# Packing 64 times of two channels on the 128 contraction rows of a Toeplitz convolution that runs beside attention

## The chip, the cores and the metric

One core of one Trainium2 chip. The metric is the device time of one execution in microseconds (us), median of several. Engines: PE is TensorE (PEld its weight loads), ACT is ScalarE, DVE is VectorE, POOL is GpSimd, SP issues DMAs. A run counts as slow when it is more than 1.5% above the fastest run of the same kernel in its session; ratios use the other, fast, runs. "L541" is line 541 of the kernel that the profile belongs to.

## The reference

Two independent parts whose outputs are joined on the last axis.

```python
# A: attention, S = 2048, D = 512, 32 heads of 16
qkv = x @ wqkv ; scores = q k^T / 4 ; p = softmax(scores) ; a = (p v) @ wo
# B: long convolution, 512 channels, 2048 times
k_shift = 4-tap causal shift convolution of k with shift_k
kv = k_shift * v
y[t, d] = sum over s <= t of kv[s, d] * ssm_k[d, t - s]  +  kv[t, d] * ssm_D[d]
b = q * y
```

`ssm_k` is about 0.05/45 in size. The convolution's own share of the output is so small that most kernels with a wrong convolution still pass the comparison.

## The kernel before

A small scheduler in the kernel's source places all instructions of the five engines by modelled times, which fixes the order of each engine's queue.

There are 2,048 blocks of 128 x 512 exponentials. ACT computes 1,836 of them in 741 ACTIVATEs over two or three PSUM banks each (L541). DVE takes the other 212 with a polynomial: one FX, three EH and one PTD instruction each. PE computes the scores (QK, L530), the products with v (L623), the projections, the convolution (L795), and short fillers in the gaps of its work (L996).

The convolution is a Toeplitz product. The filters are reversed, padded and stored in DRAM (`kz_scratch`). A load with a step of one element per partition gives each partition its own shifted window. Weights are columns of `kv`, one column for each block of 128 times.

```python
KV = sb("KV", [128, NB, C])                      # time in block, block (NB = 16), channel (C = 512)
WR = sb("WR", [128, R_W, S])                     # R_W = 12 filter rows: three slots of four channels
...
src = bass.AP(tensor=kz_ap.tensor, offset=kz_ap[4 * qd, 0].offset, ap=[[1, 128], [LKZ, 4], [1, S]])
h_wr[qd] = dma(sp, d_wr[i], WR[:, 4 * i:4 * i + 4, :], src, [h_kzw[0], dep], kb=2048)
...
for n in range(n0, n1):                          # lags, 16 for each channel
    for c in range(4):                           # four channels in the four column groups of the array
        d = 4 * qd + c
        ins = e.matmul(PS[32 * c:32 * c + NB - n, BGB, 128 * (kk % 4):128 * (kk % 4) + 128],
                       lhsT=KV[:, n:NB, d],      # up to 16 columns, 1,024 bytes apart
                       rhs=WR[:, r + c, 128 * (NB - 1 - n):128 * (NB - n)],
                       start=(n == 0), stop=(n == NB - 1), tile_position=(0, 32 * c))
```

This is 128 loads of 2,048 KB and 128 x 16 x 4 = 8,192 matmuls. `KV` starts as v (loaded by DMA) and is multiplied in place by the shifted k, 16 DVE instructions in the first 190 us.

The softmax here doesn't subtract the row's maximum and nothing guards it: scores larger than these inputs give would overflow.

Of the kernel before, what the change touches and what calls it, by code (L numbers as in the profile page):

```python
# [23 lines left out]
C = 512  # L24
NB = S // 128
# [4 lines left out]
R_W = 12  # L30
R_PT = 5
R_O = 8
R_A = 4
# [40 lines left out]
WAIT = 0.5  # L74
# [57 lines left out]
def bass_concat_heads__mha_block__ssm_conv_h3__prompt_kernel(  # L132
# [36 lines left out]
    KV = sb("KV", [128, NB, C])  # L169
# [11 lines left out]
    YB = sb("YB", [128, 2, 512])  # L181
# [77 lines left out]
    d_wr = [DmaSem(sem(f"d_wr{i}")) for i in range(R_W // 4)]  # L259
# [23 lines left out]
    for i in range(4):  # L283
        src = bass.AP(tensor=v2.tensor, offset=v2[512 * i + 384, 0].offset, ap=[[D, 128], [-128 * D, 4], [1, D]])
        h_vn.append(dma(sp, d_kv[2 + i], KV[:, NB - 4 - 4 * i:NB - 4 * i, :], src))

# [18 lines left out]
    h_kz0 = pool.op(lambda e: e.memset(KZS[:, :, S:S + PAD], 0.0))  # L305
# [5 lines left out]
    def unit_deps(u):  # L311
        if u[0] == "q":
            return h_x[u[1]] + [h_wq[min(u[2], 1)]]
        if u[0] == "k":
            return h_x[u[2]] + [h_wk[min(u[1], 1)]]
        if u[0] == "kv":
            return [h_kt[u[1] // 2], h_dg[0]]
        return h_x[u[1] // 4] + [h_wv]

    def pe_unit(u, bank, dcs=(0, 1, 2, 3)):  # L320
        kind = u[0]
        deps = [bank_free[bank]]
        mm_us, mm_run = 0.215, 0.213
        if kind == "q":
            _, qb, o = u
            deps += h_x[qb] + [h_wq[min(o, 1)]]

            def mm(e, dc):
                return e.matmul(PS[:, bank, :], lhsT=WQ[:, dc, o * 128:(o + 1) * 128], rhs=xT[:, dc, qb * 512:(qb + 1) * 512],  # L329
                                start=(dc == 0), stop=(dc == 3))  # L330
        elif kind == "k":
            _, o, sc = u
            c0 = KEYS0 if (o, sc) == (0, 0) else 0
            deps += h_x[sc] + [h_wk[min(o, 1)]]
            mm_us, mm_run = (512 - c0) / 512 * 0.215, (512 - c0) / 512 * 0.213

            def mm(e, dc):
                return e.matmul(PS[:, bank, c0:512], lhsT=WK[:, dc, o * 128:(o + 1) * 128],  # L338
                                rhs=xT[:, dc, sc * 512 + c0:(sc + 1) * 512], start=(dc == 0), stop=(dc == 3))
        elif kind == "kv":  # L340
            _, c, i = u
            deps += [h_kt[c // 2], h_kt0[c // 2], h_dg[0]]
            mm_us, mm_run = 0.27, 0.21

            def mm(e, b):
                ins = None
                for m in range(4):
                    c0 = LEFT + 128 * (4 * i + 3 - b) - m
                    ins = e.matmul(PS[:, bank, 128 * b:128 * b + 128], lhsT=KTR[c // 2][:, c % 2, c0:c0 + 128], rhs=DG[:, c, m, :],
                                   start=(m == 0), stop=(m == 3))  # L350
                return ins
        else:
            _, kt = u
            deps += h_x[kt // 4] + [h_wv]

            def mm(e, dc):
                return e.matmul(PS[:, bank, :], lhsT=xT[:, dc, kt * 128:(kt + 1) * 128], rhs=WV[:, dc, :],  # L357
                                start=(dc == 0), stop=(dc == 3))

        def fn(e):  # L360
            ins = None
            for dc in dcs:
                ins = mm(e, dc)
            return ins
        return pe.op(fn, deps, us=(0.105 + mm_us * len(dcs), 0.235 + mm_us * len(dcs)),
                     run=mm_run * len(dcs))

    def evac_unit(u, bank, h):
# [13 lines left out]
        elif kind == "kv":  # L382
            _, c, i = u
            dst = KV[:, NB - 4 - 4 * i:NB - 4 * i, 128 * c:128 * c + 128]
            src = PS[:, bank, :].rearrange("p (b d) -> p b d", b=4)
            h_kvc[c] = hh = urgent(lambda e: e.tensor_tensor(dst, src, dst, ALU.mult), [h, h_vn[i]], us=V512)  # L386
            kv_n[c] += 1
            if sum(kv_n[0:2]) == 8 and c < 2:
                load_qn(0, [h])
            if sum(kv_n) == 16:  # L390
                h_kvm[0] = h
        else:
            _, kt = u
            dst = VAF[:, kt, 0:H * VW].rearrange("p (h e) -> p h e", e=VW)[:, :, 0:DH]
            src = PS[:, bank, :].rearrange("p (h e) -> p h e", h=H)
            hh = urgent(lambda e: e.tensor_copy(dst, src), [h, h_vaf1], us=V512)  # L396
            h_v[kt] = hh
        bank_free[bank] = hh

    h_kvc = [None] * 4  # L400
    kv_n = [0] * 4
# [19 lines left out]
    def kz_store(us):  # L421
# [3 lines left out]
        wr_free.extend([(i, h_kzw[0]) for i in range(R_W // 4)])  # L425
# [340 lines left out]
    h_yb = [None]  # L766
    h_ybw = [None]
# [3 lines left out]
    def load_wr():  # L771
        while wr_free and wr_next[0] < C // 4:
            (i, dep), qd = wr_free.pop(0), wr_next[0]
            wr_next[0] += 1
            wr_slot[qd] = i
            src = bass.AP(tensor=kz_ap.tensor, offset=kz_ap[4 * qd, 0].offset, ap=[[1, 128], [LKZ, 4], [1, S]])
            h_wr[qd] = dma(sp, d_wr[i], WR[:, 4 * i:4 * i + 4, :], src, [h_kzw[0], dep], kb=2048)
# [5 lines left out]
    def conv_lags(qd, n0, n1):  # L783
        kk = qd % 8
        deps = [h_wr[qd], h_kvc[qd // 32]]
        r = 4 * wr_slot[qd]
        if kk % 4 == 0 and n0 == 0:
            deps.append(bank_free[BGB])

        def fn(e):  # L790
            ins = None
            for n in range(n0, n1):
                for c in range(4):
                    d = 4 * qd + c
                    ins = e.matmul(PS[32 * c:32 * c + NB - n, BGB, 128 * (kk % 4):128 * (kk % 4) + 128],  # L795
                                   lhsT=KV[:, n:NB, d],
                                   rhs=WR[:, r + c, 128 * (NB - 1 - n):128 * (NB - n)],
                                   start=(n == 0), stop=(n == NB - 1), tile_position=(0, 32 * c))
            return ins
        h = pe.op(fn, deps, us=(0.06 + 0.055 * (n1 - n0), 0.46 + 0.055 * (n1 - n0)),  # L800
                  run=0.054 * (n1 - n0))
        if n1 == NB:
            wr_free.append((wr_slot[qd], h))
            load_wr()
            if kk % 4 == 3:
                half = kk // 4
# [3 lines left out]
                hh = urgent(lambda e: e.tensor_copy(YB[:, half, :].rearrange("p (k i) -> p k i", k=4), src),  # L810
                            [h, h_yb[0]], slack=0.3, us=V512)
                bank_free[BGB] = h_ybw[0] = hh
        return h

    def conv_turn(b, bank):
        pbf = PS[:, bank, :].bitcast(BF16)

        def fn(e):
            ins = None
            for k in range(8):  # L820
                ins = e.transpose(pbf[:, 128 * k:128 * k + 128], YB[:, k // 4, 128 * (k % 4):128 * (k % 4) + 128],
                                  IDN[:, :])
            return ins
        h = pe.op(fn, [bank_free[bank], h_ybw[0], h_idn], us=(0.54, 0.681), run=0.43)
        h_yb[0] = h
        sl = b // 8
        yv = pbf.rearrange("p (c j) -> p c j", j=32)[:, :, 0:NB].rearrange("p c j -> p j c")
        yv = bass.AP(tensor=yv.tensor, offset=pbf[:, NB - 1:NB].offset, ap=[yv.ap[0], [-1, NB], [32, CHB]])
        qv = QN[:, :, CHB * (b % 8):CHB * (b % 8) + CHB]
        hh = urgent(lambda e: e.tensor_tensor(qv, yv, qv, ALU.mult), [h, h_qn[sl]], slack=0.3, us=V512)  # L830
        bank_free[bank] = hh
        if b % 8 == 7:
            dst = out2[:, D + 256 * sl:D + 256 * (sl + 1)].rearrange("(t p) c -> p t c", p=128)
            ho = dma(pool, d_outB[0], dst, QN[:, :, :], [hh])
            if sl == 0:
# [9 lines left out]
    early += [(130, ("kv", 1, i)) for i in range(4)]  # L845
    early += [(137, ("q", 0, 3)), (138, ("k", 3, 0)), (144, ("k", 3, 1)), (150, ("k", 3, 2)), (155, ("k", 3, 3))]
    early += [(N_EARLY - 4, ("kv", c, i)) for c in (2, 3) for i in range(4)]
# [3 lines left out]
             "left": C // 4 * NB, "t": 0.0}  # L851
# [10 lines left out]
    def next_unit(T):  # L862
# [3 lines left out]
        if st["turn"]:  # L866
            return T, ("turn", st["qd"] // 8 - 1)
# [13 lines left out]
    def unit_step(T):  # L881
# [7 lines left out]
        while True:  # L889
            free = max(pe.t, at(bank_free[bank]) + 0.13)  # L890
            if T < N_EARLY and st["turn"] and not part[0] and fits(T, free, 0.54):
                conv_turn(st["qd"] // 8 - 1, bank)
# [16 lines left out]
            if T < due and not fits(T, free, 0.54 if u[0] == "turn" else 0.645 if u[0] == "kv" else 0.535):  # L909
# [22 lines left out]
    def emit_bg(T):  # L932
# [5 lines left out]
        if not st["started"] and kv_n[0] == 4:  # L938
            st["started"] = True
        if T in tail_mm:  # L940
            assert st["qd"] == C // 4 and not st["turn"], (T, st)
# [3 lines left out]
        if st["qd"] == C // 4 and not st["turn"] and st["op"] == len(later_op):  # L945
# [3 lines left out]
        if st["turn"] and st["qd"] == C // 4:  # L949
            conv_turn(C // 32 - 1, BGB)  # L950
# [8 lines left out]
        while left > 0 and st["qd"] < wr_next[0] and kv_n[st["qd"] // 32] == 4 and at(h_wr[st["qd"]]) + WAIT <= pe.t:  # L959
            if st["turn"] and st["qd"] % 4 == 3 and st["lag"] + left >= NB:  # L960
                left = NB - 1 - st["lag"]
# [5 lines left out]
            n1 = min(n0 + left, NB)  # L967
# [4 lines left out]
            st["lag"] = n1 % NB  # L972
            if n1 == NB:
                st["qd"] += 1
                if st["qd"] % 4 == 0:
                    st["turn"] = st["turn"] or st["qd"] % 8 == 0
# [46 lines left out]
    assert state["qd"] == C // 4 and not state["turn"] and state["q"] == len(later_q) and state["op"] == len(later_op), state  # L1023
# [62 lines left out]
```

## Time and profile before

| | before |
|---|---|
| median of 3 runs | 877.91 us (877.63 to 878.13) |
| profiled span | 881.3 us, mean granted TensorE clock 0.981 |
| ACT busy in the 741 exponentials | 850.0 us |
| ACT idle before them | 16.3 us |
| filter loads | 128 x 2,048 KB, 11.5 us from issue to landing |

The page's summary of the kernel before. In part 2 the span is cut into 40 slices, digits are tenths, and GB/s is what all DMA engines moved.

```profile
span 881.3 us, 29042 instructions
...
PE 760.8 (86%) x13186; PEld 320.5 (36%) x13186; DVE 799.4 (91%) x1325; ACT 853.1 (97%) x746; POOL 17.3 (2%) x33
...
PEclk9999999999999999999999999999999879999978
DMA  9960057678999979999999999999999989999921
GB/s 281 298 262 1 29 210 249 253 258 311 405 392 397 408 302 379 391 392 403 398 406 366 386 405 355 373 402 407 407 405 379 396 320 347 407 408 406 402 98 36
```

ACT is the limit (97%). The DMA engines are the second: from the eleventh slice on they are full in nearly all slices, at about 400 GB/s. PEclk falls below 9 only in two places.

Next the queues, the chain of work that ended last (engines only), the costliest groups and the filter loads of the same page. A group reads: line, engine, operation, output<-input, count | busy us, mean ns of one | idle us before it <- what ended most of that.

```profile
q1 hardware_dynamic: 87136, 279.33, 82.9%
...
q8 instruction: 104, 1.70, 0.8%
...
ACT 52%; DVE 30%; PE 8%; DMA 6%; issue 3%; SPq 1%; ACTq 0%
...
L541 ACT ACTIVATE PT<-PS 128x1536 bf16<-128x1536 f32 (+1 forms) x741 | 850.0, 1394 | 16.3 <-PE PS L530 15.7
...
L584 DVE SCALAR_TENSOR_TENSOR EH<-EH,FX 128x512 f32<-128x512 f32 x424 | 298.1, 730 | 0.1
L795 PE MATMUL PS<-WR,KV 128*16 128x128 bf16 (+15 forms) x8192 | 231.4, 225 | 10.2 <-DMA WR<-kz_scratch 6.8
...
L795 PEld LDWEIGHTS PS<-WR,KV 128*12 128x12 bf16 (+15 forms) x8192 | 168.6, 109 | 90.3 <-issue 48.1
...
WR<-kz_scratch SPq DMA_DIRECT2D x128, 2048.0 KB, 11.5
```

Convolution matmuls wait 6.8 us in all for filter loads. Queue 8 carries 104 packets of 16 KB. The page calls its kind "instruction" and counts it, like the loads, as a share of 16 DMA engines (0.8%, the loads' queue 82.9%).

### The profile page before, as it was taken

The page shows a single profiled execution, that of the slowest core. Times are in us where ns is not written, and L with a number is a line of the kernel's source. Part 1 is how long each engine was busy: PE and PEld are TensorE (multiplying, and loading weights), DVE is VectorE, ACT ScalarE, POOL GpSimd, SP SyncE. Part 2 cuts the span into 40 slices and gives each one's busy share as a digit, 9 for nine tenths or more (in the row PEclk, how much of TensorE's full clock was granted, in tenths as well). Part 3 has the DMA queues.
Part 4 walks back from the last instruction along what each step waited for, and adds up shares of the span by engine and source line. Part 5 has one row for each costly group of instructions (what it writes and reads, how often), then busy time and mean ns, then how long its engine had stood idle before and what let it go on. Part 6 is the DMA issues. An engine that isn't in the chain of part 4 may idle for free.

```text
span 881.3 us, 29042 instructions
## 1 busy us (share of the span) xinstructions
PE 760.8 (86%) x13186; PEld 320.5 (36%) x13186; DVE 799.4 (91%) x1325; ACT 853.1 (97%) x746; POOL 17.3 (2%) x33
## 2 busy tenths in 40 slices
PE   7988999999888888888888888888888898888887
PEld 2223343443343333334333433343333334433321
DVE  3228999999999999999999999999999889999981
ACT  6999999999999999999999999999999889999986
POOL 2000000000000000000000010000000000000000
PEclk9999999999999999999999999999999879999978
DMA  9960057678999979999999999999999989999921
GB/s 281 298 262 1 29 210 249 253 258 311 405 392 397 408 302 379 391 392 403 398 406 366 386 405 355 373 402 407 407 405 379 396 320 347 407 408 406 402 98 36
DMA packets 92522, 289.31 MB, mean 328 GB/s; under 512 B 20848, under 2 KB 24944, under 8 KB 92016
## 3 DMA queue, kind: packets, MB, share of 16 engines
q1 hardware_dynamic: 87136, 279.33, 82.9%
q0 software_dynamic: 1808, 6.29, 2.1%
q8 instruction: 104, 1.70, 0.8%
q10 hardware_dynamic: 3456, 1.84, 0.8%
q14 instruction: 18, 0.15, 0.0%
HBM read 276.83 MB, written 6.42 MB: 321 GB/s over the span
## 4 chain that ended last, share of the span: by engine, by line
ACT 52%; DVE 30%; PE 8%; DMA 6%; issue 3%; SPq 1%; ACTq 0%
ACT PT L541 52%; DVE EH L584 14%; DVE FX L577 6%; DMA WR<-kz_scratch 5%; DVE PTD L589 5%; PE PS L530 3%; PE PS L623 2%; PE PS L795 1%; DVE QT L374 1%; SPq L217 1%; DVE DT L687 1%; DMA WR<-in_B_ssm_D_dram 1%; DVE YB L810 1%; DVE DTN L698 0%; PE PS L329 0%
## 5 line engine op out<-in xcount | busy, mean ns | idle before, releaser
L541 ACT ACTIVATE PT<-PS 128x1536 bf16<-128x1536 f32 (+1 forms) x741 | 850.0, 1394 | 16.3 <-PE PS L530 15.7
L530 PE MATMUL PS<-QT,KTo 32*128 32x512 bf16 x2048 | 308.1, 390 | 93.8 <-ACT PT L541 72.5
L584 DVE SCALAR_TENSOR_TENSOR EH<-EH,FX 128x512 f32<-128x512 f32 x424 | 298.1, 730 | 0.1
L795 PE MATMUL PS<-WR,KV 128*16 128x128 bf16 (+15 forms) x8192 | 231.4, 225 | 10.2 <-DMA WR<-kz_scratch 6.8
L623 PE MATMUL PS<-PT,VAF 128*32 128x512 bf16 x1836 | 204.0, 397 | 4.4 <-DVE DT L687 2.6
L795 PEld LDWEIGHTS PS<-WR,KV 128*12 128x12 bf16 (+15 forms) x8192 | 168.6, 109 | 90.3 <-issue 48.1
L530 PEld LDWEIGHTS PS<-QT,KTo 32*128 32x128 bf16 x2048 | 73.6, 91 | 272.2 <-ACT PT L541 236.2
L577 DVE TENSOR_SCALAR FX<-PS 128x512 f32<-128x512 f32 x212 | 151.8, 716 | 8.1 <-PE PS L530 7.9
L589 DVE SCALAR_TENSOR_TENSOR PTD<-EH,FX 128x512 uint16<-128x512 f32 x212 | 154.0, 728 | 0.1
L584 DVE SCALAR_TENSOR_TENSOR EH<-FX 128x512 f32<-128x512 uint16 x212 | 151.6, 730 | 0.0
L623 PEld LDWEIGHTS PS<-PT,VAF 128*32 128x32 bf16 x1836 | 48.5, 93 | 123.2 <-issue 108.7
L996 PE MATMUL PS<-IDN,ZW 128*32 128x512 bf16 (+3 forms) x234 | 76.0, 325 | 0.0
L623 PE MATMUL PS<-PTD,VAF 128*32 128x512 bf16 x212 | 60.1, 391 | 0.0
L687 DVE STREAM_TRANSPOSE DT<-PS 128x512 f32<-128x512 f32 x31 | 23.1, 744 | 18.0 <-PE PS L623 17.8
L396 DVE CAST VAF<-PS 128x512 bf16<-128x512 f32 x16 | 11.1, 691 | 27.9 <-PE PS L357 27.9
L996 PEld LDWEIGHTS PS<-IDN,ZW 128*32 128x32 bf16 x234 | 22.7, 97 | 11.5 <-issue 10.3
L374 DVE TENSOR_SCALAR QT<-PS,MASK 128x512 bf16<-128x512 f32 x30 | 21.4, 759 | 2.9 <-PE PS L329 2.4
L810 DVE CAST YB<-PS 128x512 bf16<-128x512 f32 x32 | 22.6, 707 | 1.5 <-PE PS L623 0.9
L357 PE MATMUL PS<-WKV,xT 128*128 128x512 bf16 x64 | 18.8, 384 | 3.0 <-DVE VAF L396 2.4
L740 PE MATMUL PS<-WKV,OTN 128*128 128x512 bf16 x64 | 19.7, 385 | 1.2 <-DVE OTN L709 1.2
L338 PE MATMUL PS<-xT,WKV 128*128 128x512 bf16 (+1 forms) x64 | 18.2, 377 | 1.2 <-DVE QT L374 0.6
L329 PE MATMUL PS<-xT,WQ 128*128 128x512 bf16 x60 | 18.0, 384 | 0.2 <-DVE KV L386 0.2
(62 smaller groups left out, 199.4 us busy)
## 6 DMA issues: line engine op xcount, KB each, us to landing
WR<-kz_scratch SPq DMA_DIRECT2D x128, 2048.0 KB, 11.5
kz_scratch<-WR SPq DMA_DIRECT2D x1, 2176.0 KB, 8.5
KV<-in_B_v_dram SPq DMA_DIRECT2D x4, 512.0 KB, 7.2
QN<-in_B_q_dram POOLq DMA_DIRECT2D x2, 1024.0 KB, 10.8
out_dram<-QN POOLq DMA_DIRECT2D x2, 1024.0 KB, 8.3
out_dram<-OUTA POOLq DMA_DIRECT2D x12, 128.0 KB, 5.5
QN<-in_B_ssm_k_dram SPq DMA_DIRECT2D x1, 1024.0 KB, 5.9
QT<-in_B_ssm_k_dram SPq DMA_DIRECT2D x1, 1024.0 KB, 7.8
```

The source lines that it names most:

```text
L374: lambda e, par=par: e.tensor_scalar(QT[:, qb % 2, 2 * o + par, :], PS[:, bank, :], MASK[:, par:par + 1], None, ALU.mult),
L530: ins = e.matmul(PS[:, bank, :], lhsT=KTo[32 * s:32 * s + 32, g // 2, kt * 128:(kt + 1) * 128], rhs=QT[32 * s:32 * s + 32, qb % 2, g, :], ...
L541: h_exp[T] = act.op(lambda e: e.activation(PT[:, T % R_PT, 0:n * QB], PS[:, banks[0]:banks[0] + n, :].rearrange("p b f -> p (b f)"), ACT.E ...
L577: h_f = urgent(lambda e: e.tensor_scalar(fx, PS[:, bank, :], FIX_ADD, FIX_HI, ALU.add, ALU.min), [h, h_last.get(i - R_FX)], slack=0.6)
L584: st["h"] = dve.op(lambda e: e.scalar_tensor_tensor(eh, src, (A3, A2, A1)[j], frac, ALU.add, ALU.mult), [st["h"], h_last.get(i - R_EH), h_ ...
L589: lambda e: e.scalar_tensor_tensor(out16, eh, A4, fx, ALU.mult, ALU.add),
L623: ins = e.matmul(dst, lhsT=w, rhs=rhs, start=(k == 0), stop=(k == KT - 1), tile_position=(0, 32 * s))
L687: h_t = urgent(lambda e: e.transpose(out=dt, in_=PS[:, pvb(n), :]), [h] + before, slack=0.1, us=(0.63, 0.751))
L740: ins = e.matmul(PS[:, bank, :], lhsT=OTN[:, (4 * qb + o) % R_O, t * 128:(t + 1) * 128], rhs=WO[:, o, :], start=(o == 0), stop=(o == 3))
L795: ins = e.matmul(PS[32 * c:32 * c + NB - n, BGB, 128 * (kk % 4):128 * (kk % 4) + 128], lhsT=KV[:, n:NB, d], rhs=WR[:, r + c, 128 * (NB - 1 ...
L810: hh = urgent(lambda e: e.tensor_copy(YB[:, half, :].rearrange("p (k i) -> p k i", k=4), src), [h, h_yb[0]], slack=0.3, us=V512)
L996: pe.op(lambda e: e.matmul(PS[32 * s:32 * s + 32, pvb(n), 0:128 * k], lhsT=ZW[:, :], rhs=rhs, start=False, stop=False, tile_position=(0, 3 ...
```

## The change

The intent: halve the filter bytes. Only 64 windows of each channel are loaded. Two channels, 128 apart, share the 128 rows: one on partitions 0 to 63, its partner on 64 to 127. The `kv` columns of the two channels alternate, with zeros in the other channel's half, so one matmul serves two channels. Blocks are now of 64 times, so a channel pair has 32 lags and up to 32 weight columns. The matmul count stays at 8,192.

```diff
-R_W = 12
+R_W = 10
-WAIT = 0.5
+WAIT = 1.0
...
-    KV = sb("KV", [128, NB, C])
+    KVF = sb("KV", [128, 2, 2 * NB, C // 2])
+    KV = KVF[:, :, :, :].rearrange("p r (e h) u -> p r e h u", h=2)
...
+    for h in range(2):
+        h_kv0 = pool.op(lambda e, h=h: e.memset(KV[64 * h:64 * h + 64, :, :, 1 - h, :], 0.0), [h_kv0], us=(4.5, 4.6))
...
-            src = bass.AP(tensor=kz_ap.tensor, offset=kz_ap[4 * qd, 0].offset, ap=[[1, 128], [LKZ, 4], [1, S]])
-            h_wr[qd] = dma(sp, d_wr[i], WR[:, 4 * i:4 * i + 4, :], src, [h_kzw[0], dep], kb=2048)
+            for h in range(2):
+                row = 256 * (x // NOCT) + 128 * h + 2 * (x % NOCT)
+                src = bass.AP(tensor=kz_ap.tensor, offset=kz_ap[row, 0].offset, ap=[[1, 64], [LKZ, 2], [1, S]])
+                h_wr[x] = dma(sp, d_wr[i], WR[64 * h:64 * h + 64, 2 * i:2 * i + 2, :], src, [h_kzw[0], dep])
...
-                                   lhsT=KV[:, n:NB, d],
-                                   rhs=WR[:, r + c, 128 * (NB - 1 - n):128 * (NB - n)],
+                                   lhsT=KVF[:, lag % 2, 2 * q:32, 4 * od + c],
+                                   rhs=WR[:, rows[c], w0:w0 + w],
```

Cut: the products of k and v become 32 half-partition instructions in place of 16, their shift matmuls go from 256 to 512 with half as many weight columns, the output turns are regrouped (16 fewer casts) with fewer output buffers, and the convolution starts when the first half of all products is done.

## The prediction

> **What bounds the kernel now.** ScalarE. The engine table gives ACT 853.1 us of the 881.3 us span (97%), DVE 799.4 (91%). The cost groups give 850.0 us to the 741 exponentials. By shape, their typical end-to-end steps are 0.917 us (387 of two blocks) and 1.344 us (353 of three); summed, 829 us. The span therefore holds about 35 us above this pace. The waits list shows 15.7 us of ACT waiting for the QK matmuls. In stretches of 22 us ACT loses most at 682 to 748 (6 us busy time lost) and 836 to 858 (2.6 us). There the chain of waits passes through loads of the filter rows (5% of the span) and TensorE's granted clock falls to 0.73. From 220 to 836 us the DMA share is about 1.0 at 390 to 408 GB/s: 128 loads of 2,048 KB. So DMA is the second limit and delivers 16 lags per 5.2 us, about 3.1 lags/us.
>
> **What changes.** The instruction order shows: filter bytes halve (256 loads of 512 KB); 8,192 convolution matmuls remain, but weights have up to 32 columns rather than 16; 16 fewer YB casts (-11.3 us of DVE at 707 ns), 16 more KV multiplications (+11 us); KV convolution matmuls 256 to 512 of 64 columns; exponentials stay 741, one block moves to DVE (-0.4 us of ACT). Convolution starts near the 135th exponential instead of near the 85th.
>
> **Costs.** Loads write 64 partitions each. [...] the convolution needs about 3.1 lags/us, so stalls depend narrowly on the rate (estimate: none at 210 GB/s, 11 us at 200, 36 us at 190).
>
> Strided weight loads: lag steps within a burst are 56 ns up to 13 columns, 58 ns at 15, about 63 ns at 16: about 4 ns per column beyond 14. At 32 columns I estimate 125 ns, so +0.7 us per 32 lags, +45 us of TensorE in all. Bursts hold at most six lags (+0.35 us); TensorE waits for ACT in 500-odd places (236 us on the weight loads), so most is hidden; 3 us reach ACT. Early, where TensorE is 95% busy, 1 to 2 us more. Two GpSimd memsets end before anything needs them.
>
> **On the critical path.** Removed: 8 to 12 us of DMA stalls and low-clock aftermath. Added: 3 to 5 us. ACT's 829 us stays.
>
> **Prediction: 872 us, 8 in 10 between 862 and 889. Faster by over 2%: 0.07; within 2%: 0.85; slower: 0.08.**
>
> **Right if:** ACT exponentials stay 741 and near 840 us; HBM reads about 143 MB; waits of convolution matmuls for filter loads nearly vanish; no clock dip near 700 us; loads of 512 KB move at 200 GB/s or more; convolution weight loads last longer at 32 columns and lag steps reach 110 to 130 ns.
>
> **Wrong if:** half-partition loads move under 195 GB/s (DMA share stays 1.0 at half the GB/s, stalls everywhere: 890 and more); slow bursts delay QK each time (ACT idle for QK above 25 us); or most of the 35 us came from DMA pressure, giving 855.

The cut in "Costs" is a transfer rate assumed for loads of 64 partitions, which no trace of the kernel before shows, and the conclusion from it that supply would hardly rise. 877.9 us less 8 to 12 plus 3 to 5 comes to 869 to 875, around the 872 given. That stalls for loads would go, which is the 8 to 12 us, rested on that assumed rate alone: it was my assumption.

## The result, and the profile after

| | before | after |
|---|---|---|
| median | 878.02 us (4 runs, 877.63 to 882.33) | 983.57 us (4 runs, 979.67 to 987.27) |
| ratio of fast runs | | 1.119 [1.113, 1.125] |
| profiled span, granted clock | 881.3 us, 0.981 | 985.5 us, 0.944 |
| ACT busy in exponentials / idle before them | 850.0 / 16.3 | 908.9 / 61.5 |

A ratio is the mean time of one kernel's fast runs over that of the other's fast runs of the same rounds, so it is not quite the ratio of the medians. Brackets are 95% intervals.

The changed kernel is 12% slower. Its page, the same lines as before:

```profile
span 985.5 us, 29568 instructions
...
PE 814.5 (83%) x13348; PEld 376.9 (38%) x13389; DVE 865.7 (88%) x1330; ACT 912.0 (93%) x746; POOL 32.3 (3%) x35
...
PEclk9997599999989999989799799999989999999999
DMA  9990003538788988977788798887978977776502
GB/s 262 246 203 1 1 8 97 114 87 197 169 184 200 192 180 178 205 166 172 163 191 178 167 235 201 188 182 178 206 162 189 195 169 171 175 155 145 121 2 65
```

```profile
q1 hardware_dynamic: 62624, 145.12, 66.4%
...
q8 instruction: 106, 1.74, 0.8%
...
ACT 46%; DVE 24%; PE 21%; issue 6%; SPq 1%; DMA 1%; ACTq 0%
...
L555 ACT ACTIVATE PT<-PS 128x1536 bf16<-128x1536 f32 (+1 forms) x741 | 908.9, 1424 | 61.5 <-PE PS L544 59.0
...
L598 DVE SCALAR_TENSOR_TENSOR EH<-EH,FX 128x512 f32<-128x512 f32 x426 | 320.3, 781 | 0.3
L812 PE MATMUL PS<-WR,KV 128*26 128x128 bf16 (+8 forms) x8192 | 286.2, 245 | 36.5 <-issue 35.0
L812 PEld LDWEIGHTS PS<-WR,KV 128*22 128x22 bf16 (+7 forms) x8192 | 231.9, 152 | 122.6 <-issue 100.6
...
WR<-kz_scratch SPq DMA_DIRECT2D x256, 512.0 KB, 8.7
```

The bytes did halve (279 to 145 MB on queue 1), and no convolution matmul waits for a load. Yet the DMA share is still 7 to 9 tenths at half the GB/s.

The two ACT figures split the loss. The 741 exponentials are as many as before, but they take 908.9 - 850.0 = 58.9 us longer, and ACT is idle 61.5 - 16.3 = 45.2 us longer. The sum, 104.1 us, is the growth of the span (104.2 us). So there are two questions: why do ACT's own instructions last longer, and why does it wait for PE?

**The idle half.** The waits lists of the changed kernel, PE and then ACT (us in total, times, longest):

```profile
PE PS L812 <- issue: 35.0, 26, 3.3
...
ACT PT L555 <- PE PS L544: 59.0, 82, 3.2
```

"issue" means that PE waited for nothing the profile shows. One such gap in the timeline of PE (start us, us, ..., idle before), and the DMA queues in the half microsecond in which it begins (packets, MB, share of 16 engines):

```profile
253.43 0.40 PE L637 MATMUL PS<-PT,VAF 128*32 128x512 bf16 x4
253.66 0.40 PE L812 MATMUL PS<-WR,KV 128*6 128x128 bf16 x13
256.68 0.23 PE L812 MATMUL PS<-WR,KV 128*4 128x128 bf16 x3 [2.62 <-issue]
```

```profile
q1 hardware_dynamic: 31, 0.11, 101.5%
q8 instruction: 1, 0.02, 15.9%
```

PE stops in the middle of a run of convolution matmuls whose weights and filters are all there. In the trace's packet records, one 16 KB packet of queue 8 runs from 253.78 to 255.05 us. PE goes on 1.63 us after it ended. A half-clock stretch of 3.41 us follows at 258.26 us. All 18 half-clock stretches that begin between 20 and 900 us in this trace begin 1.2 to 5.0 us after the start of a PE gap of 1.1 to 3.8 us. Of the 36 PE gaps of over 1.1 us, 16 have no such stretch.

There is one such packet for about every 253 PE instructions in the trace, and the long PE gaps sit at instruction numbers a multiple of about 253 apart. I read this as PE having run out of instructions. I counted PE gaps (from the start of one PE instruction, weight loads included, to the start of the next) of over 0.9 us that end 1.1 to 1.75 us after a queue-8 packet ended. There are 29 (49.3 us) after the change and 3 (3.2 us) before. The window is 0.65 us in a 7 to 8 us period, so of all gaps over 0.9 us about 3 of the 31 before and 5 of the 62 after would fall in by chance. Of the 29, 27 end within one stretch of 13 instructions in a period of 252.75 instructions, which chance does not give; of the other two, the one that ends at 87.1 us is a wait for DVE. I call these "fetch gaps" below. "Half clock" below is the total time that the trace shows at a granted clock of 0.5.

At the same time, the 4 KB packets of the filter loads take a median of 312 ns in place of 161, and a queue-8 packet 1.31 us in place of 1.04.

**The busy half.** I set each EH instruction of DVE against the number of convolution weight columns loaded while it ran. Before, it takes 691 ns plus 0.61 ns per column (correlation 0.72). After, the slope is 0.81 ns per column (0.92): 690 ns on average without any column, 1,163 ns with 500 to 700. The end-to-end steps of ACT without idle time behave likewise: 0.37 ns per column before (0.75) and 0.71 after (0.90), up to 0.6 us on a 1.34 us step. FX, which reads PSUM, stretches too: 0.40 ns per column before (0.49) and 0.71 after (0.89). So weight loads with strided columns seem to slow the other two engines.

**Theories.** *Loads*: loads that write only 64 neighbouring partitions hold up PE's instruction fetch; PE gaps and half clock follow. *Weights*: strided weight columns stretch ACT and DVE. The rivals were that only one of them counts, that the slower lag steps of PE (from one lag's four matmuls to the next lag's: 56 ns up to 14 columns, 124 ns at 30) delay QK, and that the late start or POOL's zeroing did it.

### The profile page after: what moved, and what is told of

The parts are those of the page before. It is cut to its first block, busy times and chain, and to the rows that moved or that the text cites. A ratio compares the mean times of both kernels' runs of the same rounds, so it can differ in the third digit from the quotient of the medians.

```text
span 985.5 us, 29568 instructions
## 1 busy us (share of the span) xinstructions
PE 814.5 (83%) x13348; PEld 376.9 (38%) x13389; DVE 865.7 (88%) x1330; ACT 912.0 (93%) x746; POOL 32.3 (3%) x35
## 3 DMA queue, kind: packets, MB, share of 16 engines
HBM read 142.61 MB, written 6.42 MB: 151 GB/s over the span
## 4 chain that ended last, share of the span: by engine, by line
ACT 46%; DVE 24%; PE 21%; issue 6%; SPq 1%; DMA 1%; ACTq 0%
ACT PT L555 46%; DVE EH L598 11%; PE PS L544 8%; PE PS L812 5%; PE PS L637 5%; DVE FX L591 4%; DVE PTD L603 4%; DVE KV L399 2%; PE PS L361 1%; DVE QT L386 1%; DVE DT L701 1%; SPq L221 1%; DMA WR<-in_B_ssm_D_dram 1%; PE PS L754 1%; PE PS L340 1%
## 5 line engine op out<-in xcount | busy, mean ns | idle before, releaser
L555 ACT ACTIVATE PT<-PS 128x1536 bf16<-128x1536 f32 (+1 forms) x741 | 908.9, 1424 | 61.5 <-PE PS L544 59.0
L598 DVE SCALAR_TENSOR_TENSOR EH<-EH,FX 128x512 f32<-128x512 f32 x426 | 320.3, 781 | 0.3
L812 PE MATMUL PS<-WR,KV 128*26 128x128 bf16 (+8 forms) x8192 | 286.2, 245 | 36.5 <-issue 35.0
L812 PEld LDWEIGHTS PS<-WR,KV 128*22 128x22 bf16 (+7 forms) x8192 | 231.9, 152 | 122.6 <-issue 100.6
L637 PE MATMUL PS<-PT,VAF 128*32 128x512 bf16 x1835 | 213.4, 409 | 13.0 <-issue 6.5
L603 DVE SCALAR_TENSOR_TENSOR PTD<-EH,FX 128x512 uint16<-128x512 f32 x213 | 163.2, 771 | 0.3
L598 DVE SCALAR_TENSOR_TENSOR EH<-FX 128x512 f32<-128x512 uint16 x213 | 160.6, 774 | 0.1
L1012 PE MATMUL PS<-IDN,ZW 128*32 128x256 bf16 (+3 forms) x245 | 81.0, 331 | 0.7 <-DVE QN L845 0.4
L399 DVE TENSOR_TENSOR KV<-PS,KV 64x512 bf16<-64x512 f32 x32 | 23.5, 733 | 3.7 <-PE PS L361 3.1
L391 DVE CAST KTo<-PS 128x512 bf16<-128x512 f32 (+1 forms) x16 | 11.7, 732 | 8.8 <-PE PS L349 8.8
## 6 DMA issues: line engine op xcount, KB each, us to landing
QN<-in_B_q_dram POOLq DMA_DIRECT2D x2, 1024.0 KB, 11.5
```

The source lines that it names most:

```text
L399: h_kvc[c] = hh = urgent(lambda e, dst=dst, src=src: e.tensor_tensor(dst, src, dst, ALU.mult), [h, h_vn[2 * c + i // 4], h_kv0], us=V512)
L555: h_exp[T] = act.op(lambda e: e.activation(PT[:, T % R_PT, 0:n * QB], PS[:, banks[0]:banks[0] + n, :].rearrange("p b f -> p (b f)"), ACT.E ...
L598: st["h"] = dve.op(lambda e: e.scalar_tensor_tensor(eh, src, (A3, A2, A1)[j], frac, ALU.add, ALU.mult), [st["h"], h_last.get(i - R_EH), h_ ...
L603: lambda e: e.scalar_tensor_tensor(out16, eh, A4, fx, ALU.mult, ALU.add),
L637: ins = e.matmul(dst, lhsT=w, rhs=rhs, start=(k == 0), stop=(k == KT - 1), tile_position=(0, 32 * s))
L812: ins = e.matmul(PS[32 * c:32 * c + 32 - 2 * q, BGB, 128 * kk:128 * kk + w], lhsT=KVF[:, lag % 2, 2 * q:32, 4 * od + c], rhs=WR[:, rows[c] ...
```

## The experiments

All profiles are of fast runs except where noted. Eighteen kernels ran. This table holds before, after and the ten runs on which the argument rests most, with ACT's figures from the same group line as above; the others are reported below. "Half" loads fill partitions 0 to 63 or 64 to 127, "all" loads fill 128 partitions, "alternate" loads every second one. "Near" weights are neighbouring columns.

| run | loads | weights | data | median us | ratio | ACT busy | ACT idle | fetch gaps | half clock us |
|---|---|---|---|---|---|---|---|---|---|
| before | all | 16, 1,024 B apart | right | 878.0 | 1 | 850.0 | 16.3 | 3, 3.2 us | 36 |
| after | half | 32, 512 B apart | right | 983.6 | 1.119 | 908.9 | 61.5 | 29, 49.3 us | 112 |
| e1 | all | 32, 512 B | wrong | 948.8 | 1.078 | 907.3 | 24.8 | 4, 4.8 us | 46 |
| e2 | half | 16, 512 B | wrong | 978.0 | 1.111 | 879.4 | 79.4 | 33, 60.4 us | 140 |
| e3 | all | 16, 512 B | wrong | 916.2 | 1.041 | 874.9 | 23.2 | 9, 10.8 us | 47 |
| e4 | half, on before | 16, 1,024 B | wrong | 892.1 | 1.014 | 849.5 | 25.2 | 10, 20.5 us | 36 |
| e5 | half | 32 near | wrong | 971.6 | 1.105 | 847.5 | 110.1 | 39, 79.4 us | 202 |
| e6 | all | 32 near | wrong | 865.8 fast, 881.4 slow | none | 834.0 | 14.6 | 7, 8.7 us | 15 |
| e12 | alternate | 32 near | wrong | 865.4 | 0.985 | 833.6 | 13.9 | 4, 4.6 us | 18 |
| e7 | all, on before | 16 near | wrong | 868.9 | 0.989 | 835.3 | 15.0 | 7, 10.9 us | 23 |
| e16 | all, on before | 16, 8 B apart | right | 876.6 | 0.998 | 835.4 | 26.0 | 5, 6.9 us | 44 |
| e18 | half, two queues | 32, 8 B apart | right | 942.7 (six runs, three slow) | 1.064 | 842.4 (slow run) | 86.3 (slow run) | 28, 54.5 us | 139 |

Reading down "ACT busy": about 908 with up to 32 strided columns, 875 to 880 capped at 16, 850 in the layout of before, 834 to 848 with near or 8-byte columns, whatever the loads do. Reading down "ACT idle": 60 to 110 with half-partition loads in the changed kernel (40 in e17 with its two queues, below), 14 to 26 with loads of all or alternate partitions. The two columns answer to two different causes.

One part of the idle time belongs to neither. In the changed kernel's profile, 30.7 of the 112 us at half clock run from 88 to 118 us, before the first convolution matmul (146.7 us) and with the DMA share at 0.00. It begins just after a PE wait of 0.84 us for DVE's FX. The same wait (0.84 to 0.85 us) stands in e1, e2, e5, e6 and e12, where 0, 20.5, 6.8, 0 and 0 us at half clock begin within 2 us of it; what makes the difference no run shows. Up to 146.7 us ACT had been idle 13.9 us, against 2.4 us in the kernel before. e1, e6 and e12 were idle 8 to 10 us in their first 150 us, with 0 to 7 us at half clock between 60 and 150 us, so most of this early idle time stays when the loads are cured.

### First set: one cause at a time

**e1_wide**: the loads alone, wrong data. Same number, same 512 KB.

```diff
-                src = bass.AP(..., ap=[[1, 64], [LKZ, 2], [1, S]])
-                h_wr[x] = dma(sp, d_wr[i], WR[64 * h:64 * h + 64, 2 * i:2 * i + 2, :], src, ...)
+                src = bass.AP(..., ap=[[1, 128], [1, S]])
+                h_wr[x] = dma(sp, d_wr[i], WR[:, 2 * i + h, :], src, ...)
```

> The changed kernel with each filter load of 64 partitions x 2 rows turned into one of 128 partitions x 1 row: same 256 loads, same 512 KB each, same waits and the same instruction order; the results are wrong on purpose. Theory A (TensorE runs dry because its instruction fetches queue behind 4 KB packets that take about 310 ns instead of 160 ns when only half the partitions are written): packets back near 165 ns, fetch packets near 1.05 us, the 20-odd TensorE gaps over 1.2 us that follow a fetch all but vanish, the 14 clock dips after 250 us go, time 900 to 915 us. Theory B (32-column weight loads stretch the bursts and hold up QK): loads do not matter, time stays 970 to 985 us.

Measured: 948.79 us (2 runs), ratio 1.078 [1.069, 1.086], in between. The packets went to 159 ns, the fetch gaps fell from 29 to 4, and a third of the loss came back. The ACT and DVE groups of its page did not improve:

```profile
L555 ACT ACTIVATE PT<-PS 128x1536 bf16<-128x1536 f32 (+1 forms) x741 | 907.3, 1445 | 24.8 <-PE PS L544 23.3
...
L598 DVE SCALAR_TENSOR_TENSOR EH<-EH,FX 128x512 f32<-128x512 f32 x426 | 328.0, 803 | 0.3
```

Idle time is nearly cured (61.5 to 24.8), busy time is untouched. So the loads explain the idle half and nothing of the busy half.

**e2_narrow**: the weights alone, capped at 16 columns (`q = max(q, 8)` ahead of the matmul), so that the output is wrong.

```diff
                for c in range(4):
+                    q = max(q, 8)
                     ins = e.matmul(PS[32 * c:32 * c + 32 - 2 * q, ...], lhsT=KVF[:, lag % 2, 2 * q:32, 4 * od + c], ...)
```

> The changed kernel with its half-partition loads, but never more than 16 weight columns in a convolution matmul (results wrong on purpose; number and length of matmuls unchanged). Theory A: gaps after instruction fetches stay, [...] time 950 to 985 us. Theory B: lag steps go back to 56-63 ns, ACT stops waiting for QK in the middle of the run, time 890 to 905 us.

Measured: 977.96 us (2 runs), ratio 1.111 [1.101, 1.121], within the first range. ACT busy falls by 29.5 us, which the first theory did not contain, and ACT's idle time rises by 17.9 us, which hides it.

**e3_wide_narrow**: both edits together; wrong output again.

> Both edits together, wrong on purpose. Both theories: what is left over 878 us is the early stage (slower start and half-clock stretch before 130 us, about 15 us in the changed kernel's trace), so 880 to 895 us. If it is far above that, a third cause acts in the long middle.

Measured: 916.24 us (2 runs), ratio 1.041 [1.032, 1.050], a miss. Together the edits give back 67 us, against 35 and 6 alone, but ACT's instructions still take 25 us longer than before. Counting weight columns over all 8,192 loads: 69,632 before, 139,264 after, and still 102,400 in this run, which shortens only the weight loads of more than 16 columns. A cap can't take the columns' cost away while they are strided, so I turned to the stride.

**e4_before_half**: the kernel before, each load made into two of 64 partitions x 2 rows (half the bytes, wrong data).

```diff
-            src = bass.AP(..., ap=[[1, 128], [LKZ, 4], [1, S]])
+            for h in range(2):
+                src = bass.AP(..., offset=kz_ap[4 * qd + 2 * h, 0].offset, ap=[[1, 64], [LKZ, 2], [1, S]])
+                h_wr[qd] = dma(sp, d_wr[i], WR[64 * h:64 * h + 64, 4 * i:4 * i + 2, :], src, ...)
```

> The kernel before, with each filter load of 128 partitions x 4 rows replaced by two of 64 partitions x 2 rows: half the bytes, the same number and size of loads as the changed kernel, each row used twice; results wrong on purpose, compute untouched. Theory A: packets take about 310 ns, the wait of instruction fetches grows by 1 to 2 us, gaps after fetches and clock dips appear, time 910 to 960 us. Theory B: with half the bytes and unchanged weights it is as fast as before or faster, 865 to 880 us.

Measured: 892.11 us (2 runs), ratio 1.014 [1.006, 1.021]. The packets are as slow as after the change (309 ns) and fetch gaps appear (10, 20.5 us), but the cost is about 12 us (before took 880.33 us in the same session), less than the theory said; by the 2% rule the verdict is "unclear". The same loads do more harm in the changed kernel. Why is only partly known; see "What stays open".

**e5_contig**: the changed kernel with near columns (wrong data), loads as changed.

```diff
-                                   lhsT=KVF[:, lag % 2, 2 * q:32, 4 * od + c],
+                                   lhsT=KVF[:, lag % 2, 31, 4 * od:4 * od + 32 - 2 * q],   # other end for the last channels
```

> The changed kernel, only the weight address differs: the same number of weight columns per convolution matmul, read from neighbouring elements instead of 512 bytes apart (wrong values on purpose; same instruction order, half-partition loads kept). Theory C ([...] the traces so far give about 0.7 to 0.8 ns of stretch per column loaded during an instruction, r about 0.9): lag steps back to 56 ns, DVE steps of EH back to a mean near 700 ns, ACT steps without idle time lose under 10 us in the middle; fetch gaps stay, so 930 to 955 us. Theory B' (it is the column count, whatever the stride): as the changed kernel, 975 to 985 us.

Measured: 971.56 us (2 runs), ratio 1.105 [1.094, 1.117], slower than expected. From its page:

```profile
PEclk9998999998888779788989678889888798999998
...
L555 ACT ACTIVATE PT<-PS 128x1536 bf16<-128x1536 f32 (+1 forms) x741 | 847.5, 1287 | 110.1 <-PE PS L544 107.4
...
L598 DVE SCALAR_TENSOR_TENSOR EH<-EH,FX 128x512 f32<-128x512 f32 x426 | 280.6, 679 | 0.3
```

The stretch is gone: EH takes 679 ns with a slope of zero against columns, and the lag steps of PE are 56 to 57 ns at every column count. But ACT idles 110 us. Fetch gaps rose to 39 (79.4 us) and the half clock to 202 us, and what was saved went there.

**e6_contig_wide**: e5 with the loads of e1.

> The same neighbouring weight columns plus loads of 128 partitions x 1 row. Theories A and C together explain all of the long middle: 885 to 897 us, what is left being the early stage; no fetch gaps, no stretch. If it is above 905 us, another cause remains.

Measured: 865.76 us in a fast run and 881.36 in one that counts as slow, beside 876.09 to 880.94 for before; better than expected. One fast run is thin, but e8 (869.42) and e12 (865.38) agree with it. Both causes gone, the loss is gone: about 110 us, of which taking away the loads alone gave back 35 and the weights alone 12. This also takes the late start of the convolution out of question, since it is as late here.

**e7_before_contig**: the kernel before with near columns (wrong data).

```diff
-                                   lhsT=KV[:, n:NB, d],
+                                   lhsT=KV[:, 15, d:d + NB - n],    # other end for the last channels
```

> The kernel before with neighbouring weight columns (wrong values on purpose, everything else the same). Theory C: it, too, pays for strides, with up to 16 columns about 12 us of stretch in the middle; 862 to 873 us. Theory B': no change, 876 to 882 us.

Measured: 868.9 us (2 runs), ratio 0.989 [0.981, 0.997], as expected. The strided weights cost the kernel before too: ACT busy 850.0 to 835.3.

**e8_late_zero**: e6 with POOL's zeroing moved behind the store of the filters.

```diff
-        h_kv0 = pool.op(lambda e, h=h: e.memset(KV[64 * h:64 * h + 64, :, :, 1 - h, :], 0.0), [h_kv0], ...)
 ...
         h_kzw[0] = dma(sp, d_kzw, kz_ap.rearrange("(p c) m -> p c m", c=4), KZS, [h, h_kz0], kb=2176)
+        zero_kv(h)                                 # the same two memsets, now behind h
```

> The contiguous, full-width kernel with the GpSimd zeroing of the weight tile moved behind the filter copies of VectorE, so that the two do not overlap near 10 to 18 us. If the zeroing blocks the VectorE copy (it took 3.4 us for two in the changed kernel, 1.3 us before) and so starts the early loss: first 60 us lose about 3 us less, 3 to 5 us faster than the run without it. If the early loss has its own cause in the KV units: no difference over 2 us.

Measured: 869.42 us (2 runs), ratio 0.989 [0.980, 0.998]. ACT's loss in the first 60 us fell from 6.3 to 2.1 us, but half-clock stretches appeared near 100 and 140 us. The zeroing is no cause of any size.

### Second set: what is it about the loads, and do the cures work with right data?

**e9_merged**: right data. Each load fills one row of all 128 partitions by a source of two outer steps.

```diff
+                src = bass.AP(..., ap=[[128 * LKZ, 2], [1, 64], [1, S]])
+                h_wr[x] = dma(sp, d_wr[i], WR[:, 2 * i + r, :], src, [h_kzw[0], dep])
```

> The changed kernel with correct data: each pair of filter loads that filled partitions 0 to 63 and then 64 to 127, two rows each, becomes two loads that each fill one row of all 128 partitions (64 windows of one channel, then 64 of its partner). Same number of loads, same 512 KB each, same bytes, same results. Theory (a load that writes to only 64 neighbouring partitions is slow and holds up TensorE's instruction fetch): packets near 160 ns instead of 312, fetch gaps from 29 to under 10, time as with the wrong-data wide loads, 949 us, range 935 to 960. Rival (the wide loads of the earlier run gained by reading 128 windows of one single row of the scratch, not by the partitions): packets stay near 300 ns and the time near 983.

Measured: 2,711.45 us (4 runs), ratio 3.08 [3.07, 3.09]. The packets were fast (161 ns), but the page's queue line shows why that did not help:

```profile
q1 hardware_dynamic: 59040, 145.10, 14.0%
```

14.0% of 16 engines is the work of about two, and the mean rate was 57 GB/s. The outermost dimension of the source is 2 here and in e10 (13.5%), where the other filter loads have 64 or 128. That this decides how many engines work is my reading; no run varies it alone. The run says nothing about either theory.

**e10_merged_contig**: e9 with near columns and v staged elsewhere.

```diff
+    KVT = sb("KV", [128, 2, C // 2, 2 * NB])
+    VS = WRF[:, 6 * S:10 * S].rearrange("p (c r n d) -> p c r n d", c=2, r=2, n=NB)    # v
...
-                                   lhsT=KVF[:, lag % 2, 2 * q:32, 4 * od + c],
+                                   lhsT=KVT[:, lag % 2, 4 * od + c, 2 * q:32],
```

> Correct data. The changed kernel with both causes taken away: loads as in the merged run, and the product of k and v laid out with the 32 block columns of a channel next to each other, so that the weights are neighbouring columns. v is staged in the last four filter rows, so two of the five slots become free only at about 200 us. Theory: EH near 680 ns without a slope against weight columns, lags at 56 ns, few fetch gaps; time as in the wrong-data run with both causes gone, 873 us, range 862 to 888, that is within 2 per cent of the kernel before. Rival (the wrong-data run gained by something its wrong weights did, for instance reading the same few columns again and again): 900 or more.

Measured: 2,795.57 us (4 runs), ratio 3.18 [3.17, 3.19], for the same reason as e9; inconclusive on the time. EH had no slope against columns here either (0.004 ns per column).

**e12_interleave**: e5 with only the destination of the loads changed, from the lower and upper half to even and odd partitions (wrong data).

```diff
-WR[64 * h:64 * h + 64, 2 * i:2 * i + 2, :]
+WR[h:128:2, 2 * i:2 * i + 2, :]
```

> Wrong data on purpose. The run with neighbouring weights and half-partition loads (971.6 us), with only the destination of each load changed: 64 partitions in steps of two (all even, all odd) instead of the lower and the upper half. If it is the side of the memory that counts (which partitions one load writes to), packets fall from 312 to about 160 to 200 ns, fetch gaps fall from 39 to under 10, time 865 to 890. If it is the number of partitions of one load, or the two rows per partition, packets stay at about 310 ns and the time at 955 to 985.

Measured: 865.38 us (4 runs), ratio 0.985 [0.981, 0.989], against 971.56 for e5. Its page:

```profile
PEclk9699999999999999999999999999999999999999
...
L555 ACT ACTIVATE PT<-PS 128x1536 bf16<-128x1536 f32 (+1 forms) x741 | 833.6, 1381 | 13.9 <-PE PS L544 13.3
...
WR<-kz_scratch SPq DMA_DIRECT2D x256, 512.0 KB, 6.2
```

Same partition count, rows, bytes, number of loads and instruction streams as e5. Only which 64 partitions one load writes differs: packets 159 ns, fetch gaps 4, and 106 us less. This settles the loads' part. It is not the number of partitions but which ones. Why writes to 64 neighbouring partitions are slower than writes to 64 alternate ones, no run shows.

Since e5 and e12 have the same instruction stream, the queue-8 packets can also be compared against a fixed place in it: they start 2.5 to 3.6 us later in e5 on average, depending on the place chosen. What delays them no run shows.

**e11_before_turned**: right data. The kernel before with `KV` laid out `[128, C, NB]`, so that the columns of a channel are neighbours. v is staged in the third filter slot, which is free only at about 200 us.

```diff
-    KV = sb("KV", [128, NB, C])
+    KVT = sb("KV", [128, C, NB])
+    KV = KVT[:, :, :].rearrange("p d n -> p n d")
+    VS = WRF[:, 8 * S:12 * S].rearrange("p (n d) -> p n d", n=NB)    # v
...
-                                   lhsT=KV[:, n:NB, d],
+                                   lhsT=KVT[:, d, n:NB],
```

> Correct data. The kernel before with only the layout of the product of k and v turned, so that the weights of a channel are neighbouring columns; v staged in the last four filter rows, so the third slot becomes free only at about 200 us. Theory (strided weights also cost the kernel before something): EH slope against weight columns gone, 730 to about 680 ns, time 864 to 873 us, ratio 0.983 to 0.995. Rival (the gain of the wrong-data version was from something else): 877 or more.

Measured: 913.08 us (6 runs), ratio 1.040 [1.036, 1.043], a miss. The stretch was gone (EH 681 ns, ACT busy 841.2), but the write of the turned product had become slow, 2,334 ns in place of about 690:

```profile
L389 DVE TENSOR_TENSOR KV<-PS,WR 128x512 bf16<-128x512 f32 x16 | 37.3, 2334 | 4.9 <-PE PS L351 4.9
```

### Third set: a correct version

**e13_pool_turn**: e11 without its two suspects. v is staged a quarter at a time in buffers idle then, so all slots are free from the start. DVE writes in natural order, and POOL turns the layout.

```diff
+            hh = urgent(lambda e: e.tensor_tensor(vs, src, vs, ALU.mult), [h, h_vn[c]], us=V512)
+            h_kvc[c] = hv = pool.op(lambda e: e.tensor_copy(dst, vs), [hh], us=(3.0, 3.1))
```

> Correct data. The kernel before with neighbouring weight columns, but without the two costs suspected in the 913 us version: v is staged a quarter at a time in the buffers of the output rows and of the v weights, which are idle then, so that all three slots of filter rows are free from the start as before; and DVE writes the product of k and v in natural order into that staging buffer (about 680 ns each, as before) while POOL, idle otherwise, turns it into the layout with neighbouring columns. Theory (neighbouring weights do help with correct data; the 913 us version lost its gain to the slow turned writes and the late third slot): 864 to 874 us, ratio 0.983 to 0.995, EH near 680 ns, no PE waits for filter loads over 3 us in total. Rival (neighbouring weights don't help once the data are right): 880 or more.

Measured: 911.46 us (6 runs), ratio 1.039 [1.035, 1.042], a miss on the time, though ACT busy was 840.8. Twenty microseconds by stretch (busy us of each engine, granted clock, DMA share, GB/s), the kernel before and then e13:

```profile
90.00:100.00 10.00, 8.95 (x99) 3.46 (x95) 9.74 (x17) 9.79 (x11) 0.00 (x0) 1.00 0.01 2
100.00:110.00 10.00, 9.50 (x113) 3.09 (x114) 9.65 (x17) 10.00 (x10) 0.00 (x0) 1.00 0.18 59
```

```profile
90.00:100.00 10.00, 6.83 (x46) 2.23 (x43) 9.44 (x12) 7.03 (x7) 5.54 (x2) 0.67 0.00 0
100.00:110.00 10.00, 7.34 (x60) 2.80 (x60) 8.93 (x13) 4.66 (x5) 3.69 (x2) 0.50 0.00 0
```

POOL is copying, DVE is "busy" with fewer instructions, PE falls idle, its clock halves for 27 us, and ACT runs at half. Thirteen of the 28 EH instructions that overlapped one of POOL's 2.4 to 2.9 us copies took 1.2 to 2.3 us in place of 683 ns. None of the 13 FX instructions did. EH takes its inputs from SBUF and FX from PSUM; whether that makes the difference, no run separates.

**e14_dve_turn**: as e13, DVE writes the turned layout itself.

```diff
-            hh = urgent(lambda e: e.tensor_tensor(vs, src, vs, ALU.mult), [h, h_vn[c]], us=V512)
-            h_kvc[c] = hv = pool.op(lambda e: e.tensor_copy(dst, vs), [hh], us=(3.0, 3.1))
+            h_kvc[c] = hh = hv = urgent(lambda e: e.tensor_tensor(dst, src, vs, ALU.mult), [h, h_vn[c]], us=V512)
```

> Correct data. As the run with POOL turning, with one thing put back: DVE itself writes the turned layout, 16 times about 2.33 us in place of 0.68. The third slot is free from the start. If the slow turned writes made most of the loss of the 913 us version: 890 to 905. If the late third slot did: 868 to 882. Both about equally: 882 to 890.

Measured: 907.6 us (4 runs), ratio 1.035 [1.031, 1.039], just above the first range. Putting the slow writes back alone kept most of e11's loss; the late slot made about 5 us of it (913.1 to 907.6). By 250 us ACT had lost 39 us against its typical steps (4 in the kernel before), in half-clock stretches after PE had waited for those writes.

**e15_stride8**: the kernel before, weight columns 8 bytes apart (wrong data). What is the cost of a stride paid for?

```diff
-                                   lhsT=KV[:, n:NB, d],
+                                   lhsT=KV[:, 15, d0 + 4 * n:d0 + 4 * NB:4],    # d0 = min(d, C - 4 * NB)
```

> Wrong data on purpose. The kernel before, with the weight columns of one load 8 bytes apart (4 elements) in place of 1024; all else as it is. [...] EH slope about half of 0.61 ns per column, time about 872 to 876. If any stride other than neighbouring columns costs the same: slope 0.6, time 876 to 880. If only strides far above 8 bytes cost: slope under 0.1, time as with neighbouring columns, 865 to 872.

Measured: 872.25 us (4 runs), ratio 0.994 [0.990, 0.998]. The EH slope is 0.005 ns per column and the ACT slope 0.001, so columns 8 bytes apart disturb as little as neighbours. The slope was the third expectation ("under 0.1"); the time fell in the range of the first. The slope is the direct reading.

**e16_groups4**: right data. `KV` as `[128, C // 4, NB, 4]`: columns of a channel 8 bytes apart, DVE writes runs of four.

```diff
-    KV = sb("KV", [128, NB, C])
+    KV4 = sb("KV", [128, C // 4, NB, 4])
...
-                                   lhsT=KV[:, n:NB, d],
+                                   lhsT=KV4[:, d // 4, n:NB, d % 4],
```

> Correct data. The kernel before with the product of k and v laid out in groups of four channels, so that the weight columns of a channel are 8 bytes apart and DVE writes runs of four elements; v staged as in the two runs before, all slots free from the start. If the turned write is paid per run (1650 ns for 512 runs of one element): 0.68 + 0.41 = about 1.1 us for each of the 16 writes, no half-clock stretch of 20 us before 250 us, and the time 868 to 882. If a write in runs of four is as slow as one in runs of one (2.33 us): 895 to 910.

Measured: 876.56 us (6 runs), ratio 0.998 [0.994, 1.001]: the same as before, within the first range. The tile view (min/median/max ns) shows that a write in runs of four costs nothing extra, not even the 1.1 us expected:

```profile
L389 DVE TENSOR_TENSOR KV<-PS,OUTA x8: 683/691/704, 81.7 to 164.9; 128x512 bf16<-128x512 f32 x8
```

ACT busy is 835.4, but idle rose from 16.3 to 26.0 us, and PE waits 17.8 us for filter loads in place of 6.8. With ACT faster, the full DMA is the next limit.

**e17_two_queues**: the changed kernel, right data, loads of the upper half issued by POOL into its own queue, with semaphores of their own.

```diff
-                h_wr[x] = dma(sp, d_wr[i], WR[64 * h:64 * h + 64, 2 * i:2 * i + 2, :], src, ...)
+                h_wr[(x, h)] = dma(pool if h else sp, d_wr[h][i], WR[64 * h:64 * h + 64, 2 * i:2 * i + 2, :], src, ...)
```

> Correct data. The changed kernel with one thing moved: of each pair of filter loads, the one for partitions 64 to 127 is issued by POOL into its own queue, so that a load for the lower half and one for the upper half can be under way at the same moment. Strided weights as they are. If it is the side written to at any one moment that counts, the packets get faster and the time falls to that of the wide loads, about 949 us, range 930 to 965. If a load to one half is slow whatever runs beside it: 975 to 995. If the issue by POOL itself disturbs DVE, EH without weight columns rises above 700 ns and the time stays above 965.

Measured: 976.67 us (4 runs, one slow), ratio 1.105 [1.098, 1.112], within the second range. The profile is of the fastest run (964.94). In it the packets' median fell from 312 to about 250 ns, the fetch gaps to 10 and ACT's idle time to 40.4 us. EH without weight columns took 702 ns, but also 698 in e1, so the third expectation is not told apart. By the time of the kernel the second queue gains almost nothing (976.67 against 983.57 us); by its packets, a fifth shorter, it gains something.

**e18_two_queues_groups4**: right data, e17 with groups of four.

```diff
+    KV4 = sb("KV", [128, 2, C // 8, 2 * NB, 4])
...
-                                   lhsT=KVF[:, lag % 2, 2 * q:32, 4 * od + c],
+                                   lhsT=KV4[:, lag % 2, od, 2 * q:32, c],
```

> Correct data. The changed kernel with both causes treated: the two queues, and the product of k and v in groups of four channels, so that the weight columns are 8 bytes apart. If both treatments work: 862 to 885, a ratio of 0.98 to 1.01, against 874 and 865 for the wrong-data versions with wide or alternate-partition loads and neighbouring columns. If the two queues don't help: 955 to 985, as with neighbouring weights alone.

Measured: 942.74 us (6 runs, three of them slow; the profile is of a slow one); ratio of the fast runs 1.064 [1.057, 1.070], better than the second expectation and far from the first. Without the weights' stretch the fetch gaps came back (28), as in e5.

No correct version beat the kernel before. e16 equals it. The wrong-data runs e7, e6 and e12 show that about 11 to 14 us against before of the same session are there (under 2%, and one fast run for e6) if a layout gives near columns, with loads over all or alternate partitions. For the changed kernel that needs two channels on alternate partitions with right data, which I did not build: the products of k and v would have to be written to every second partition.

## Why the prediction was wrong

It said 872 us (862 to 889) and gave "slower" 0.08. It was 983.57.

**Right.** Bytes, counts and the load rate: HBM reads 142.61 MB ("about 143"), 741 exponentials, loads at about 200 GB/s ("200 GB/s or more"; 16 engines at 4,096 bytes in 312 ns make 210), waits of the convolution for filter rows gone, lag steps 124 ns at 30 columns ("110 to 130"). The vanished waits are partly luck: the slowed convolution asked for only 2.5 lags/us (2,048 lags in 812 us), not the 3.1 that the prediction set against the supply.

**First failed step: "TensorE waits for ACT in 500-odd places [...] so most is hidden; 3 us reach ACT."** I costed the strided weight loads on PE alone, and there they are hidden. What they do to the others was left out: 0.71 ns of ACT and 0.81 ns of DVE for each strided column, with ACT the limit. The prediction let 3 us of delay reach ACT and left ACT's own instructions as long as they were. Measured: ACT busy +58.9 us; gone with near columns at either kind of load (e5, e6), and with 8-byte columns (e16 on the kernel before, e18 on the changed one). The sign was in the profile before: EH at 730 ns, with a slope of 0.61 ns per column. I took it for the price of the instruction.

**Second failed step: "the convolution needs about 3.1 lags/us, so stalls depend narrowly on the rate".** I let slow loads act only through convolution matmuls that wait for filters. Those waits did vanish. The loads acted on something outside the kernel's data flow: packets of 312 ns in place of 161 beside queue-8 packets of 1.31 us in place of 1.04, then fetch gaps, then the half clock (36 to 112 us, of which 34 us lie before the convolution and are not explained by this). Measured: ACT idle +45.2 us, 11.5 us of it before the first convolution matmul; e1 took 36.7 us of it away with the loads alone, and e12 took away 96 us against e5 by the choice of partitions alone. That it is the instruction fetch is inferred from the timing of queue 8; that it is the loads, and which partitions they write, is shown.

**"Wrong if" named two signs.** "DMA share stays 1.0 at half the GB/s" came close (0.7 to 0.9). "ACT idle for QK above 25 us" came true (59.0). I gave them 0.08 because I thought of each only through the waits of the convolution.

**Why the parts don't add.** Taking away one cause gave back 35 us (e1) or 12 us (e5), both about 110. My reading: with near columns, PE runs through its instructions faster and meets the slow fetch more often (measured: 39 gaps, 202 us of half clock). With the fetch cured, ACT is still held by its own stretched instructions. So a single undo undercounts both.

**What stays open.** The same half loads cost the kernel before about 12 us (e4) and the changed one far more; the later start, the closer pacing and the smaller products of k and v all differ, and no run separates them. The half clock from 88 to 118 us and the early idle time of ACT have no shown cause. How a strided weight load reaches into ACT and DVE is not shown, only that it does. Nor is its price one number: a column costs ACT 0.37 ns in the kernel before, 0.54 in e2 and e3 (512 bytes apart, at most 16 columns) and 0.71 with up to 32.

## What to carry to other kernels

Before halving a load's bytes by halving its partitions, check which partitions it writes: here, 64 alternate ones were as good as 128 (865.4 us in e12, 865.8 in e6), and 64 neighbouring ones cost 106 us in the same program (971.6 in e5). Cost an operand's stride on every engine that runs at the same time and not only on the one that reads it, and look for a layout that keeps the elements of the walk close: 8 bytes apart were free here (0.005 ns of EH per column), 512 and 1,024 were not (0.81 and 0.61), and nothing between was tried. When an engine idles on "issue" at regular distances in its instruction stream, look at the instruction queue beside the DMA load; and when two causes feed each other, undo both before judging either.
